# Six column blocks of a gated layer formed while attention still runs, with their results in slots and the score banks in rings of three

## The chip, the cores and the metric

The kernel runs on one core of a Trainium2 chip. The metric is device time in microseconds. The kernel before took 649.47 us as the median of three runs (643.34 to 655.79).

## The reference

```python
scores = 1/sqrt(64) * q @ k.T                  # 2 batches, 12 heads, 448 tokens, 64 wide
attn = softmax(causal(scores)) @ v             # row maximum subtracted, sum + 1e-9
x = attn as 896 tokens x 768
xn = x / sqrt(mean(x * x) + 1e-6) * rms_g
g, val = xn @ w_gate, xn @ w_val               # 768 x 1536, float64
y = (g * sigmoid(g) * val) @ w_out             # 1536 x 768
h = y @ w_in                                   # 768 x 2048
out = maximum(0.01 * h, h) @ w_out2            # 2048 x 768
```

The inputs q, k and v are float32. The weights arrive as float64 and are split on the chip.

## The kernel before, in words

**Attention.** The heads go in twelve pairs; pairs 0 to 5 are the first half of the tokens (b = 0, 448 tokens), pairs 6 to 11 the second (b = 1). For each pair `maxima` forms score products (L281) and VectorE reduces each row block to its maximum (L289); `maxima_rows` transposes the maxima (L315) and sends them through DRAM to one row of `mrow` (L320, L324). Two pairs later `exponents` forms the transposed scores minus the maximum (L339, L343), ScalarE takes the exponential (L364), and GpSimd masks it (L370, L374). `attend` forms the sums of the exponentials (L401, into the bank SM) and the products with v (L386, into the bank AV). The sums travel through DRAM to be inverted on 64 partitions (L423, L427, L431, L434) and come back broadcast (L436, L441); GpSimd multiplies (L448), ScalarE squares (L456), and GpSimd adds the squares up in `acc` (L459). The eight banks of PSUM are two for the maxima (SP), four for the exponents (ST), AV and SM.

**Norm.** `norm(b)`, once per half, sums the squares over partitions on TensorE (L477), takes the power on GpSimd (L493), spreads the result over all partitions by four products (L484), copies it to `rsb` (L500), and scales and splits the six row blocks of the half into a rounded part and a rest (L504, L507, L514 or L510). The two parts are `xn`.

**Weights.** `weight` loads one block of 128 columns as float64 (768 KB, L182, a ring of three buffers `raw`), rebuilds the float32 on ScalarE and VectorE (L187, L188, L190, L192, L194, a ring of two buffers `x`), rounds it (L196), and leaves the rest to GpSimd (L197), in a ring of four `hl`. Every product of the three layers is three passes of 128x128 by 448 columns: rounded by rounded, rounded by rest, rest by rounded (L573, L574, L575).

**The gated layer.** Twelve column blocks fc, each with a weight for g and one for val, are formed for both halves (`gate`: 18 matmuls for one weight and one half). `gate_out` takes Silu (L625), multiplies (L627), rounds (L630) and subtracts (L632) into T. The products of fc 0 and 1 for b = 0 (`EARLY = 2`) stand among the last pairs of attention; their `gate_out` waits for the buffers of attention to be given up (`reopen`), as T lies in that memory. Then come y (L669 and after), G (L699 and after) and the output.

**What sets the order.** `Order.add` takes every step with an engine, a cost, its reads and writes, and a rank. `emit` places steps one after another: on the engine that is free first, the ready step of lowest rank, with 6 added for a change of the matmul mode. The result is one fixed list for each engine, that of SyncE among them, which issues all DMAs. On the chip every engine works its list strictly in order, so a step that waits holds up all steps behind it on its engine.

## Time and profile before

| | before |
|---|---|
| median of three runs | 649.47 us |
| the profiled execution | 649.4 us, its span 647.7 us |
| TensorE busy | 623.2 us, 96% of the span |
| VectorE, ScalarE, GpSimd busy | 393.6, 250.1, 196.1 us |
| mean granted clock of TensorE | 0.968 of full speed |
| bytes moved | 68.24 MB, of which 64.78 MB read |

A profile row for an instruction has its start, its length, engine and line, what it writes and reads, how many of its kind are merged, and in square brackets the idle time of the engine before it with what ended it. A row of the stretches has the stretch, its length, and the busy time and count of each engine, the granted clock of TensorE and the load of the DMA engines.

### The profile page before, as it was taken

How to read it: one execution, taken by the hardware profiler on the slowest of the kernel's cores; microseconds unless marked ns; L12 is line 12 of the kernel's file. 1: busy time of each engine (PE TensorE's matmuls, PEld its weight loads, DVE VectorE, ACT ScalarE, POOL GpSimd, SP SyncE). 2: the span in 40 equal slices, each digit the busy share in tenths (PEclk: the TensorE clock that was granted, in tenths of full speed). 3: DMA queues.
4: the chain of work that ended last, by engine and by line, in shares of the span. 5: the costliest groups of instructions: out<-in, count | busy, mean ns of one | idle time of the engine just before them, and what ended most of it. 6: DMA issues, size and time to landing. Idle time of an engine off the chain costs nothing.

```text
span 647.7 us, 8644 instructions
## 1 busy us (share of the span) xinstructions
PE 623.2 (96%) x3280; PEld 537.4 (83%) x3280; DVE 393.6 (61%) x668; ACT 250.1 (39%) x410; POOL 196.1 (30%) x158
## 2 busy tenths in 40 slices
PE   7987888997999999999999999999999999999997
PEld 4554466566989999999999999999999999999997
DVE  5567443625798776655674554599999883444300
ACT  3564442632543433333333223345554543223210
POOL 0154333843233322223232222232233223232300
PEclk9887876998999999999999999999999999999999
DMA  6353221131145233333233223233233333434000
GB/s 241 126 186 102 83 78 32 30 119 60 50 146 190 104 102 130 112 124 118 97 109 135 98 98 101 95 117 127 99 98 87 125 97 115 140 112 143 29 28 28
DMA packets 20177, 68.24 MB, mean 105 GB/s; under 512 B 5092, under 2 KB 8104, under 8 KB 20136
## 3 DMA queue, kind: packets, MB, share of 16 engines
q1 hardware_dynamic: 20136, 67.70, 31.4%
q8 instruction: 25, 0.41, 0.2%
q14 instruction: 16, 0.13, 0.1%
HBM read 64.78 MB, written 2.91 MB: 105 GB/s over the span
## 4 chain that ended last, share of the span: by engine, by line
PE 90%; DVE 3%; issue 3%; DMA 3%; POOL 1%; ACT 1%; SPq 0%; POOLq 0%; DVEq 0%; ACTq 0%
PE bank L573 25%; PE bank L575 25%; PE bank L574 25%; PE bank L386 4%; PE bank L343 3%; PE bank L401 2%; PE bank L281 2%; PE bank L339 2%; DVE bank L289 1%; DMA st<-sd 1%; PE bank L524 1%; POOL hl L197 1%; DVE x L504 1%; PE bank L484 0%; DMA rb<-rd 0%
## 5 line engine op out<-in xcount | busy, mean ns | idle before, releaser
L197 POOL TENSOR_TENSOR hl<-x,hl 128x768 fp32r<-128x768 f32 (+1 forms) x70 | 138.7, 1981 | 334.8 <-ACT hl L196 329.2
L573 PE MATMUL bank<-xn,hl 128*128 128x448 f32 x288 | 106.9, 371 | 2.2 <-ACT xn L507 1.9
L574 PE MATMUL bank<-xn,hl 128*128 128x448 f32 x288 | 106.3, 369 | 1.3 <-POOL xn L514 0.8
L575 PE MATMUL bank<-xn,hl 128*128 128x448 f32 x288 | 106.1, 368 | 0.8 <-POOL hl L197 0.8
L187 ACT ACTIVATE x<-raw 128x768 f32<-128x768 f32 (+1 forms) x70 | 61.7, 883 | 105.1 <-POOL hl L197 105.1
L188 DVE TENSOR_SCALAR x<-x 128x768 f32<-128x768 f32 (+1 forms) x70 | 39.1, 559 | 93.6 <-ACT x L187 93.6
L192 DVE SCALAR_TENSOR_TENSOR x<-raw,x 128x768 uint32<-128x768 uint32 (+1 forms) x70 | 85.0, 1215 | 2.3
L196 ACT CAST hl<-x 128x768 fp32r<-128x768 f32 (+1 forms) x70 | 56.8, 812 | 53.3 <-PE bank L574 44.9
L574 PE MATMUL bank<-y,hl 128*128 128x448 f32 x192 | 70.1, 365 | 0.0
L573 PE MATMUL bank<-G,hl 128*128 128x448 f32 x192 | 70.1, 365 | 0.0
L575 PE MATMUL bank<-G,hl 128*128 128x448 f32 x192 | 70.1, 365 | 0.0
L573 PE MATMUL bank<-y,hl 128*128 128x448 f32 x192 | 70.1, 365 | 0.0
L575 PE MATMUL bank<-y,hl 128*128 128x448 f32 x192 | 70.1, 365 | 0.0
L574 PE MATMUL bank<-G,hl 128*128 128x448 f32 x192 | 70.1, 365 | 0.0
L194 DVE SCALAR_TENSOR_TENSOR x<-raw,x 128x768 uint32<-128x768 uint32 (+1 forms) x70 | 65.1, 929 | 1.1
L573 PEld LDWEIGHTS bank<-xn,hl 128*128 128x128 f32 x288 | 54.8, 190 | 7.7 <-ACT xn L507 2.1
L289 DVE CUSTOM_DVE_ANT_0 bank<-bank,maskw 112x224 f32<-112x224 f32 (+2 forms) x96 | 42.0, 466 | 31.4 <-PE bank L281 30.2
L574 PEld LDWEIGHTS bank<-xn,hl 128*128 128x128 f32 x288 | 54.6, 190 | 6.6 <-POOL xn L514 1.3
L575 PEld LDWEIGHTS bank<-xn,hl 128*128 128x128 f32 x288 | 54.7, 190 | 5.5 <-POOL hl L197 1.2
L573 PE MATMUL bank<-T,hl 128*128 128x448 f32 x144 | 52.6, 365 | 0.0
L575 PE MATMUL bank<-T,hl 128*128 128x448 f32 x144 | 52.6, 365 | 0.0
L574 PE MATMUL bank<-T,hl 128*128 128x448 f32 x144 | 52.6, 365 | 0.0
(79 smaller groups left out, 927.7 us busy)
## 6 DMA issues: line engine op xcount, KB each, us to landing
raw<-in_out SPq DMA_DIRECT2D x24, 768.0 KB
raw<-in_in SPq DMA_DIRECT2D x16, 768.0 KB
raw<-in_gate SPq DMA_DIRECT2D x12, 768.0 KB
raw<-in_val SPq DMA_DIRECT2D x12, 768.0 KB
qk<-in_qk SPq DMA_DIRECT2D x12, 448.0 KB
v<-in_v SPq DMA_DIRECT2D x12, 256.0 KB
raw<-in_out SPq DMA_DIRECT2D x6, 512.0 KB
out<-sg SPq DMA_DIRECT2D x12, 224.0 KB
```

The lines of the kernel that those rows point to most:

```text
L187: add("ACT", 0.85, lambda: nc.scalar.activation(x[:, :w], tf, AF.Abs), r=[kr], w=[kx], rank=rank)
L188: add("DVE", 0.62, lambda: nc.vector.tensor_scalar(x[:, :w], x[:, :w], LEAST, MOST, ALU.max, ALU.min), r=[kx], w=[kx], rank=rank)
L192: add("DVE", 1.0, lambda: nc.vector.scalar_tensor_tensor(xb, top, 0xC0000000, xb, ALU.bitwise_and, ALU.bitwise_or), r=[kr, kx], w=[kx], ra ...
L194: add("DVE", 1.0, lambda: nc.vector.scalar_tensor_tensor(xb, low, 29, xb, ALU.logical_shift_right, ALU.bitwise_or), r=[kr, kx], w=[kx], ra ...
L196: add("ACT", 0.85, lambda: nc.scalar.copy(hl[:, 0, :w], x[:, :w]), r=[kx], w=[kh], rank=rank)
L197: add("POOL", 1.95, lambda: nc.gpsimd.tensor_tensor(out=hl[:, 1, :w], in0=x[:, :w], in1=f32(hl[:, 0, :w]), op=ALU.subtract), r=[kx, kh], w ...
L289: nc.vector.tensor_tensor_reduce(out=s, in0=s, in1=maskw[:, S - w:S], scale=-1.0, scalar=3.0e38, op0=ALU.add, op1=ALU.min, accum_out=m[:, ...
L343: nc.tensor.matmul(bank[:k1 - kb * P, off:off + w], t[r, 1, kb * P:k1], t[r, 0, kb * P:], start=False, stop=True, skip_group_check=True,)
L386: nc.tensor.matmul(AV[j * D:(j + 1) * D, kb * P:S], vt[:, kb, j], p, start=kb == 0, stop=kb == KB - 1, skip_group_check=True,)
L573: nc.tensor.matmul(o, hi, xh, start=s, stop=False, skip_group_check=True)
L574: nc.tensor.matmul(o, hi, xl, start=False, stop=False, skip_group_check=True)
L575: nc.tensor.matmul(o, lo, xh, start=False, stop=e, skip_group_check=True)
```

## The change

The gated layer forms six column blocks instead of two for the first half of the tokens early (`EARLY = 6`), in the banks 4 and 5, and finishes them at once: their `gate_out` no longer waits for attention's memory, as the six results have slots of their own (`big`), and its last step goes to GpSimd. T and G become lists of such slots of one column block and one half; y overwrites `xn`. To make room, the ring `raw` has two buffers instead of three, the rings of q, k and v four instead of five, and `x32` is a ring of eight blocks of 448 columns. `norm(0)` is issued after pair 6 instead of pair 7, with a lower rank for its scaling. Pairs 0 to 5 use three banks for the maxima and three for the exponents; pairs 6 to 11 two and two, which leaves banks 4 and 5 to the gates. As the ring of split weights holds four, the weights of fc 0 to 3 are loaded and split a second time for b = 1, after fc 11 (`again`): 78 blocks are split instead of 70. The number of products is the same: 2953 rows of TensorE's order before and after.

```diff
-    NRAW, NX, NHL = 3, 2, 4
+    NRAW, NX, NHL = 2, 2, 4
...
-    xn = xyp.tile([P, 2, KD, NT], F32R, tag="xy", name="xn")
-    late = {}
...
+    xn = xyp.tile([P, 2, KD, NT], F32R, name="xn")
+    y = xn
...
+    EARLY = 6
+    NBIG = B * KF2
+    big = [xyp.tile([P, 2, S], F32R, name=f"big{n}") for n in range(EARLY)]
+    sgs = [xyp.tile([P, S], F32, name=f"sg{n}") for n in range(2)]
+    order = [(fc, 0) for fc in range(EARLY)]
+    order += [(fc, b) for fc in range(KF) for b in range(B) if (fc, b) not in order]
+    t_slot = {k: n for n, k in enumerate(order)}
+    unused = list(range(len(order), NBIG)) + list(range(len(order)))
+    g_slot = {(fc, b): unused[fc * B + b] for fc in range(KF2) for b in range(B)}
...
-    for fc in range(KF):
-        queue += [(("g", fc), w_gate[fc]), (("v", fc), w_val[fc])]
+    for fc in list(range(KF)) + list(range(EARLY - 2)):
+        again = len(queue) >= 2 * KF
+        queue += [(("g", fc, again), w_gate[fc]), (("v", fc, again), w_val[fc])]
...
-    NQ, NR, NM, NB = 5, 3, 4, 4
+    NQ, NR, NM, NB = 4, 3, 4, 4
...
-    x32 = ap.tile([P, KD, NT], F32, name="x32")
+    NX32 = 8
+    x32 = ring(NX32, [P, S], F32, "x32_")
...
-    SP, ST, AV, SM = banks[0:2], banks[2:6], banks[6], banks[7]
+    AV, SM = banks[6], banks[7]
...
+    maxima_banks = [0, 1, 2], [0, 1]
+    exponent_banks = [3, 4, 5], [2, 3]
+    taken = {}
+    def take(lists, i):
+        use = lists[i >= NP]
+        n = taken.get((use[0], len(use)), 0)
+        taken[use[0], len(use)] = n + 2
+        return [use[(n + j) % len(use)] for j in range(2)]
...
-            use = [(spn[0] + j) % 2 for j in range(2)]
-            spn[0] += 2
+            use = take(maxima_banks, i)
...
-            use = [(stn[0] + j) % 4 for j in range(2)]
-            stn[0] += 2
+            use = take(exponent_banks, i)
...
-        x = x32[:, hp, b * S:(b + 1) * S]
+        x = x32[i % NX32]
...
-        u0, u1 = stn[0] % 4, (stn[0] + 1) % 4
-        stn[0] += 2
-        B0, B1 = ST[u0], ST[u1]
+        n = 0 if b else 4
+        B0, B1 = banks[n:n + 2]
+        k0, k1 = ("bank", n), ("bank", n + 1)
...
-            x = x32[:, i, b * S:(b + 1) * S]
+            n = (b * NP + i) % NX32
+            x = x32[n]
...
-                r=["rs"], w=[("x", b, i)], rank=rank + i + 30)
+                r=["rs"], w=[("x32", n)], rank=rank + i)
...
+    def bank_key(n):
+        return {6: "av", 7: "sm"}.get(n, ("bank", n))
+    def next_bank():
+        turn[0] += 1
+        return (turn[0] + 5) % 8
+            xh, xl = src(ks, b)
...
+    def of_T(k, b):
+        return [big[t_slot[k, b]][:, e] for e in range(2)]
...
+    def gate(nm, fc, b, rank, bank=None, again=False):
+        gate_bank[nm, fc, b] = u = next_bank() if bank is None else bank
+        product(u, (nm, fc, again), of_xn, six, b, True, True, rank, xn_keys(b))
...
+    def gate_out(fc, b, rank, room, lower):
+        s = next_sg()
+        ug, uv = gate_bank["g", fc, b], gate_bank["v", fc, b]
+        n = t_slot[fc, b]
+        def view(e):
+            return big[n][:, e]
+        add("ACT", 0.57, lambda: nc.scalar.activation(sgs[s], banks[ug][:, :S], AF.Silu),
+            r=[bank_key(ug)], w=[("sg", s)], rank=rank)
+        add("DVE", 0.65, lambda: nc.vector.tensor_tensor(
+            out=sgs[s], in0=banks[uv][:, :S], in1=sgs[s], op=ALU.mult),
+            r=[bank_key(uv)], w=[("sg", s)], rank=rank)
+        add("ACT", 0.57, lambda: nc.scalar.copy(view(0), sgs[s]),
+            r=[("sg", s)] + room, w=[("big", n)], rank=rank)
+        add(*lower, lambda: (nc.gpsimd if lower[0] == "POOL" else nc.vector).tensor_tensor(
+            out=view(1), in0=sgs[s], in1=f32(view(0)), op=ALU.subtract),
+            r=[("sg", s)], w=[("big", n)], rank=rank)
...
-    EARLY = 2
-    HEAD = [k for k, _ in queue[:2 * EARLY]]
-    for n, key in enumerate(HEAD):
-        weight(key, 40.0 + 10 * n, at=20.0 + 8 * n)
+    def early_rank(fc):
+        return 10.0 * (NP + 3 + fc) + 9
+    def early_weights(fc):
+        for n, nm in enumerate("gv"):
+            weight((nm, fc, False), early_rank(fc) - 12, at=40.0 + 8 * (2 * fc + n))
+    for fc in range(NHL // 2):
+        early_weights(fc)
...
-            if i in (NP + 1, NPAIR - 1):
-                norm(i // NP - (i < NPAIR - 1))
...
+            if i == NP:
+                norm(0)
+                for fc in range(EARLY):
+                    for n, nm in enumerate("gv"):
+                        gate(nm, fc, 0, early_rank(fc), bank=4 + n)
+                    gate_out(fc, 0, early_rank(fc) - 10, [], ("POOL", 1.15))
+                    if fc + NHL // 2 < EARLY:
+                        early_weights(fc + NHL // 2)
+    norm(1)
...
+        big.extend(bigp.tile([P, 2, S], F32R, name=f"big{n}") for n in range(EARLY, NBIG))
...
+    held = [k for k in list(od.written) if k not in ("const", ("bank", 4), ("bank", 5))
+            and k[0] not in ("hl", "raw", "x", "big", "sg")]
+    add("X", 0.0, reopen, r=held, w=["room"])
+    for again in (False, True):
+        for fc in range(EARLY - 2) if again else range(EARLY - 2, KF):
+            rank = FF + 2 + fc + (KF if again else 0)
+            kept = fc < EARLY and not again
+            if not kept:
                 for nm in "gv":
+                    weight((nm, fc, again), rank - 1)
+            for b in range(1 if kept or again else 0, B):
+                for nm in "gv":
+                    gate(nm, fc, b, rank, again=again)
+                gate_out(fc, b, rank, ["room"], ("DVE", 0.7))
...
```

The names in the rows of the order are the tiles of the kernel with the number of the buffer; an `ISA` row of L289 or L313 is a reduction to the row maximum, and the one behind it with only `m` reads out its result.

TensorE around the second norm (L484 before, L506 after: the four products that spread the inverse root over the partitions). Before:

```order
L575 MATMUL bank3_76<-xn_81,hl3_72 128x448
L484 MATMUL bank5_78<-dg0_152,ones_147 128x112
L484 MATMUL bank5_78<-dg1_153,ones_147 128x112
L484 MATMUL bank5_78<-dg2_154,ones_147 128x112
L484 MATMUL bank5_78<-dg3_155,ones_147 128x112
L573 MATMUL bank4_77<-xn_81,hl0_69 128x448
```

After, with 45 matmuls on the weights in hl0 to hl3 between the last L506 and the last row, which is the first product of the second half:

```order
L506 MATMUL bank1_73<-dg3_167,ones_159 128x112
L561 MATMUL bank4_76<-xn_80,hl0_68 128x448
...
L563 MATMUL bank4_76<-xn_80,hl2_70 128x448
L561 MATMUL bank5_77<-xn_80,hl3_71 128x448
L562 MATMUL bank5_77<-xn_80,hl3_71 128x448
L563 MATMUL bank5_77<-xn_80,hl3_71 128x448
L561 MATMUL bank6_78<-xn_80,hl0_68 128x448
```

Before, the product behind the spread is one of the second half. Now products of the first half with the blocks fc 4 and 5 stand between.

VectorE at the maxima of pair 4, with steps of a weight's rebuilding (L188, L190) and the inverse of pair 1's sums (L431, L434) between them. Before:

```order
L289 ISA bank1_74,m0_104<-bank1_74,maskw_149 112x336
L289 ISA m0_104 112x1
L188 TENSOR_SCALAR x0_67<-x0_67 128x768
L190 TENSOR_SCALAR x0_67<-x0_67 128x768
L289 ISA bank0_73,m0_104<-bank0_73,maskw_149 112x224
L289 ISA m0_104 112x1
L431 SCALAR_TENSOR_TENSOR r1_131<-st1_127 64x14
L434 RECIPROCAL r1_131<-r1_131 64x14
L289 ISA bank0_73,m0_104<-bank0_73,maskw_149 112x112
```

After, at the maxima of pair 8:

```order
L207 SCALAR_TENSOR_TENSOR x0_66<-raw0_64,x0_66 128x768
L313 ISA bank0_72,m0_109<-bank0_72,maskw_161 112x336
L313 ISA m0_109 112x1
L313 ISA bank1_73,m0_109<-bank1_73,maskw_161 112x336
L313 ISA m0_109 112x1
L209 SCALAR_TENSOR_TENSOR x0_66<-raw0_64,x0_66 128x768
L203 TENSOR_SCALAR x1_67<-x1_67 128x768
L205 TENSOR_SCALAR x1_67<-x1_67 128x768
L207 SCALAR_TENSOR_TENSOR x1_67<-raw1_65,x1_67 128x768
L313 ISA bank0_72,m0_109<-bank0_72,maskw_161 112x224
```

The rebuilding of weights has left the maxima of pairs 0 to 5. Six blocks are now rebuilt between the maxima of pair 6 and the scaling of the first norm, where none was.

ScalarE from the copies of pair 9's products on (L443 copies sums, L468 the products with v, L604 is Silu, L609 the rounding behind it, L386 the exponential, L202 and L211 are steps of a weight). After:

```order
L468 COPY x32_1_150<-bank6_78 128x448
L604 ACT_TABLE_LOAD
L604 ACTIVATE sg1_88<-bank4_76 128x448
L211 CAST hl0_68<-x0_66 128x768
L202 ACTIVATE x0_66<-raw0_64 128x768
L211 CAST hl1_69<-x1_67 128x768
L609 CAST big0_81<-sg1_88 128x448
L386 ACT_TABLE_LOAD
L386 ACTIVATE p0_121<-bank2_74 128x320
L386 ACTIVATE p1_122<-bank3_75 128x320
```

Before, one table load stood ahead of the first Silu, behind all exponentials. Now Silu comes between exponentials: there are five loads at L604 and L386 in place of the one at L625.

## Rows read from the trace of the kernel before

**Rows 1.** Stretches of the span: busy time of each engine, granted clock, DMA load.
```profile
40.00:64.00 24.00, 19.00 (x142) 11.98 (x142) 17.08 (x50) 14.44 (x28) 12.16 (x17) 0.88 0.43 130
64.00:116.00 52.00, 46.33 (x311) 28.94 (x303) 23.35 (x100) 21.55 (x46) 19.58 (x28) 0.79 0.23 66
...
124.00:155.00 31.00, 31.00 (x220) 23.24 (x219) 7.56 (x19) 8.53 (x19) 15.66 (x23) 1.00 0.29 101
155.00:164.00 9.00, 5.73 (x16) 4.11 (x15) 7.42 (x9) 4.88 (x8) 4.46 (x3) 0.62 0.00 0
...
180.00:640.00 460.00, 459.21 (x2266) 425.27 (x2265) 293.95 (x371) 167.84 (x254) 128.74 (x65) 1.00 0.32 108
```

**Rows 2.** Timeline of TensorE around the second norm.
```profile
154.22 1.04 PE L484 MATMUL bank<-dg,ones 112*128 112x112 f32 x8
157.19 0.74 PE L573 MATMUL bank<-xn,hl 128*128 128x448 f32 x1 [1.94 <-ACT xn L507]
...
163.91 0.39 PE L573 MATMUL bank<-xn,hl 128*128 128x448 f32 x1
```

**Rows 3.** Timeline of TensorE in the first half of attention: its waits.
```profile
7.30 2.63 PE L281 MATMUL bank<-qkr 64*112 64x336 f32 x6 [0.91 <-DVE m L289]
...
32.81 0.95 PE L281 MATMUL bank<-qkr 64*112 64x256 f32 x4 [0.66 <-DVE m L289]
...
49.95 0.26 PE L315 MATMUL bank<-ident,m 112*8 112x112 f32 x1 [2.54 <-DVE m L289]
...
62.33 0.35 PE L315 MATMUL bank<-ident,m 112*8 112x112 f32 x1 [2.46 <-DVE m L289]
```

**Rows 4.** Chain of waits: the copy ahead of the first of these two waits.
```profile
43.61 4.81 DMA st<-sd
```

**Rows 5.** Timeline of VectorE ahead of the second of them.
```profile
56.87 1.37 DVE L188 TENSOR_SCALAR x<-x 128x768 f32<-128x768 f32 x1
58.28 1.38 DVE L190 TENSOR_SCALAR x<-x 128x768 uint32<-128x768 uint32 x1
59.69 0.96 DVE L192 SCALAR_TENSOR_TENSOR x<-raw,x 128x768 uint32<-128x768 uint32 x1
```

**Rows 6.** Stretches of 4 us around the two waits.
```profile
48.00:52.00 4.00, 2.05 (x19) 1.27 (x23) 3.42 (x12) 0.75 (x2) 0.63 (x2) 0.91 0.29 75
52.00:56.00 4.00, 4.00 (x30) 1.74 (x22) 0.96 (x5) 1.94 (x3) 1.09 (x1) 0.66 0.50 181
...
60.00:64.00 4.00, 1.67 (x9) 0.69 (x13) 3.83 (x16) 1.30 (x3) 1.55 (x4) 0.69 0.23 23
64.00:68.00 4.00, 4.00 (x24) 1.45 (x18) 1.11 (x6) 0.53 (x1) 2.82 (x2) 0.50 0.46 159
```

**Rows 7.** Groups of instructions on VectorE, shapes apart: busy, mean ns | idle before.
```profile
L192 DVE SCALAR_TENSOR_TENSOR x<-raw,x 128x768 uint32<-128x768 uint32 x64 | 80.9, 1264 | 2.1
...
L194 DVE SCALAR_TENSOR_TENSOR x<-raw,x 128x768 uint32<-128x768 uint32 x64 | 60.9, 952 | 0.9
...
L190 DVE TENSOR_SCALAR x<-x 128x768 uint32<-128x768 uint32 x64 | 39.8, 623 | 1.4
L188 DVE TENSOR_SCALAR x<-x 128x768 f32<-128x768 f32 x64 | 36.6, 572 | 83.4 <-ACT x L187 83.4
...
L627 DVE TENSOR_TENSOR sg<-bank,sg 128x448 f32<-128x448 f32 x24 | 14.9, 620 | 35.5 <-PE bank L575 33.9 <-ACT sg L625 1.6
L632 DVE TENSOR_TENSOR T<-sg,T 128x448 fp32r<-128x448 f32 x24 | 14.8, 616 | 1.5 <-ACT T L630 1.5
```

**Rows 8.** Timeline of ScalarE at the first Silu.
```profile
162.46 0.56 ACT L507 CAST xn<-x 128x448 fp32r<-128x448 f32 x1 [0.57 <-DVE x L504]
163.04 1.28 ACT L625 ACT_TABLE_LOAD   x1
164.34 0.55 ACT L625 ACTIVATE sg<-bank 128x448 f32<-128x448 f32 x1
```

**Rows 9.** Waits of TensorE from 124 us on: total, times, longest.
```profile
PE bank L575 <- POOL hl L197: 0.8, 1, 0.8
```

More of the change, by code (lines that the diff above doesn't have):

```diff
@@ L300, in products @@
                     for j in range(2):
-                        product(j, c, SP[use[j]], 256 * n)
+                        product(j, c, banks[use[j]], 256 * n)
             cost = sum(max(256, (c + 1) * C) * 0.00045 + 0.05 for c in group)
-            add("PE", cost, products, r=[("qkr", i % NR)], w=[("sp", u) for u in use],
+            add("PE", cost, products, r=[("qkr", i % NR)], w=[("bank", u) for u in use],
                 rank=10 * i - 29, mode=64)
```

189 lines of the change are left out of this document (67 added, 122 removed).

## The prediction

> **What bounds the kernel now.** I read the stretches first, then the timeline of TensorE, then what ended its waits. From 180 to 640 us TensorE is busy 459.2 of 460 us at a granted clock of 1.00, with 2266 matmuls: 0.203 us for each [rows 1]. Nothing is to be had there but by fewer matmuls, and their number stays. The stretch from 124 to 155 us, in which the last pairs of attention and the four early products stand, is full too: 31.00 of 31.00 at 1.00 [rows 1]. So the place into which the change puts more early products has no hole. A product that is put there only pushes other work back, and time is won where TensorE idles or runs slowly. That is in two places: the 9 us behind the second norm (5.73 busy, clock 0.62) and the attention ahead of 116 us, with clock 0.88 from 40 to 64 us and 0.79 from 64 to 116 us [rows 1].
>
> **The gap behind the second norm.** The spread ends at 154.22 + 1.04 = 155.26, and at 163.91 the pace is normal again; twelve matmuls lie between [rows 2]. At 0.203 us they need 2.4 of these 8.65 us, so 6.2 us are lost: first waiting for the split rows of the second half, then at the low clock. In the new order 45 products of the first half stand there, 45 x 0.203 = 9.1 us, and the split rows were all used 8.65 us behind the spread. So the cover suffices, narrowly for the last rows and amply for the first, which are wanted first. I take all of it: **-6.2**, with bounds 0 and -6.2 (a spread that is itself late would not shrink it, but a scaling that queues behind a weight on VectorE could leave part).
>
> **The front: what goes.** In the first six pairs TensorE waits four times for a reduction that frees one of the two banks of maxima, 0.66 to 0.91 us, together 3.0 [rows 3]. A third bank, with other products between, takes these away. Then come two longer waits, 2.54 and 2.46 us [rows 3]. Ahead of the first, the inverse of a pair's sums waits on VectorE for a small copy that took 4.81 us [rows 4], and the reductions stand behind it; ahead of the second VectorE works at a weight for 1.37, 1.38 and 0.96 us [rows 5] before it comes to the reduction. After both the clock falls: 0.91 and 0.66, then 0.69 and 0.50 of full speed in stretches of 4 us [rows 6], 0.50 being the level of 1.2 GHz. What this takes is 4 x (0.09 + 0.34) = 1.7 and 4 x (0.31 + 0.50) = 3.2 us. So the first event cost 4.3, the second 5.7, together 10.0 us, with four weights rebuilt in the stretch. Weights now come only from pair 6 on. What goes: 3.0 + 10.0 = 13.0.
>
> **The front: what comes.** Six weights are rebuilt between the maxima of pair 6 and the scaling of the first norm. One takes VectorE 0.572 + 0.623 + 1.264 + 0.952 = 3.41 us [rows 7], six 20.5. From 64 to 116 us VectorE was busy 23.35 of 52 us [rows 1]; with them it is 43.8, or 84%, more than the 17.08 of 24 (71%) of the stretch in which the two events fell. There is room, but not for steps that come in an unlucky order. At the price of before, 10.0 / 4 = 2.5 each, six cost 15.0; only two of the four were followed by such a wait, so a weight may cost nothing. I take the middle, 7.5, since this stretch loses a fifth of its clock already and can't lose the same time twice. The two banks for exponents in pairs 6 to 8, where no gate fills in, I price by the nearest row, a ring of two that makes TensorE wait 0.66 us [rows 3]: 3 x 0.66 = 2.0. The front: -13.0 + 7.5 + 2.0 = **-3.5**, with bounds -13.0 and +4.0.
>
> **Later attention.** Four more table loads come onto ScalarE between the exponentials of the last two pairs; one took 1.28 us [rows 8], four 5.1. Two of them return to the exponential, and at one of these TensorE has little between the products and their use; I take one load: **+1.3**, bounds 0 and 5.1. The row shows the Silu 0.02 us behind the load and the load 0.02 us behind the instruction before. The Trainium skill, "ScalarE: Activation LUTs", section "What ACT_TABLE_LOAD costs", has a drain of 1.38 us with every load, 2.66 us in all; this case's row does not show it, and four such switches would be an estimated 10.6 us of ScalarE in place of 5.1.
>
> Eight loads of weights now stand in SyncE's list among the small copies of pairs 2 to 7, each waiting for VectorE to be done with the block two before. If one holds the copies up as at 43.61 us, it costs 4.3; if the buffer is free in time, nothing. I take half of one: **+2.1**, bounds 0 and 34.
>
> **The gated layer after attention.** One wait of 0.8 us for a weight [rows 9] goes, since the weights are no longer held until attention ends: **-0.8**. Eight blocks are split again. For one such column block VectorE needs 2 x 3.41 + 0.62 + 0.62 = 8.1 us [rows 7], and TensorE 36 x 0.203 = 7.3. The four split blocks in the ring cover the difference; without that cover it would be 4 x 0.8 = 3 us. The ring `raw` of two, the finish on GpSimd and the slots I cost at nothing: ahead of each weight lies 7.3 us of products or more, and in the second half GpSimd was busy 15.66 of 31 us [rows 1].
>
> **The sum**, against the profiled execution's own 649.4 us, which is also the median shown (649.47): 649.4 - 6.2 - 3.5 + 1.3 + 2.1 - 0.8 = 642.3. I forecast **642 us**, 7 us less.
>
> **Rivals.**
> A. *The front becomes dense.* The six weights fit into VectorE's idle time and the later terms vanish: 642.3 - 7.5 - 1.3 - 2.1 = 631. For it: VectorE idled 28.7 of 52 us there. Against it: the same should have held from 40 to 64 us.
> B. *The change does not do what it says.* The early products fill no idle time, because the stretch was full, and the front keeps its length as other waits take over from those that go. Only the gap is won: 642.3 + 3.5 = 646. For it: most of the front's loss lies at 64 to 116 us (52 x 0.21 = 11 us of clock, 5.7 of idle time), where no weight was rebuilt.
> C. *SyncE's list becomes the bound* (slower). In place of the weights' price and the half event, each of the eight loads delays the copies behind it by one event of 4.3: 642.3 - 7.5 - 2.1 + 34 = 667. From the fourth load on that does so the kernel is slower than before, from the seventh by over 2%. For it: one of the four loads of before did this [rows 4]. Against it: no other wait of TensorE from 40 to 64 us ended on a copy.
> D. *Table loads on the path.* If TensorE waits through all four, 642.3 + 5.1 - 1.3 = 646. By the Trainium skill's figure, same page and section, it would be an estimated 652.
>
> **Chances.** The forecast 0.50 (its own range 636 to 649), A 0.20, B 0.15, C 0.10, D 0.05. The range from 630 to 654 leaves out most of C, the low tail of A and little else, about 2 in 10. A measurement of this kernel tells 2% from no change, 13 us: below 636.5 is faster, above 662.5 slower. Faster: nearly all of A and a tenth of the forecast, 0.25. Slower: most of C, 0.08. Within 2%: 0.67.
>
> **What the profile after would show.** The gap: no wait at the first product of the second half, and a clock of 1.00 there. The front: no wait over 1 us at the transposes of pairs 4 and 5, and pair 5 done well before 62 us. The weights' price: VectorE's rebuilding steps ahead of the reductions of pairs 6 to 10, with TensorE waiting behind them. Table loads: ScalarE's row of exponents behind a load, with TensorE's next product waiting for it. I am wrong if the clock in the last four pairs of attention falls below 1.00, for then the fixed order has brought waits into a stretch that had none, or if the front shrinks by more than 13 us.

## The result, and the profile after

The changed kernel takes 652.3 us (median of 14 runs, 649.6 to 660.3); the kernel before took 646.2 beside it (14 runs, 642.5 to 657.0). The ratio is 1.011, with a 95% interval from 1.007 to 1.015: 1.1% slower, where I had forecast 1.1% faster. The comparisons leave disturbed executions out; the profiled ones of e3, e15 and e16 (spans 657.6, 656.5 and 653.2 us) are disturbed, so only the places of waits are read from them.

The profiled execution after took 649.6 us, its span is 647.8 us. It is the fastest of its 14 runs, while that of before (649.4) lies 3 us above its median. The two traces are therefore equally long: they show how time moved from one stretch to another, and not the 6 us by which the medians differ.

The stretches of the kernel after, in the columns of [rows 1], with 148 to 152 us added:

```profile
40.00:64.00 24.00, 20.78 (x161) 11.25 (x161) 13.35 (x43) 12.81 (x24) 8.82 (x13) 0.93 0.53 175
64.00:116.00 52.00, 45.39 (x269) 25.83 (x271) 39.97 (x104) 27.11 (x54) 28.73 (x33) 0.84 0.46 147
124.00:155.00 31.00, 29.30 (x162) 22.03 (x159) 22.57 (x24) 21.90 (x34) 21.25 (x16) 0.94 0.29 94
...
148.00:152.00 4.00, 4.00 (x18) 2.88 (x16) 3.23 (x5) 2.17 (x4) 2.29 (x1) 0.64 0.41 133
...
155.00:164.00 9.00, 9.00 (x59) 6.78 (x58) 5.80 (x8) 4.43 (x7) 6.56 (x7) 1.00 0.30 113
180.00:640.00 460.00, 456.35 (x2250) 422.14 (x2249) 322.50 (x384) 173.16 (x261) 138.97 (x71) 1.00 0.34 112
```

From 124 to 155 us, full at a clock of 1.00 before, TensorE now has waits (29.30 of 31.00) and a clock of 0.94; VectorE has 22.57 us of work there where it had 7.56, ScalarE 21.90 for 8.53. From 180 to 640 us 2.9 us of TensorE are missing against before.

The timeline of TensorE after, some of its waits in the middle of attention and those around the second norm (they answer to [rows 2, 3]):

```profile
49.66 0.41 PE L362 MATMUL bank<-mrow,onesr 64*128 64x320 f32 x1 [1.88 <-ACT p L386]
66.32 0.95 PE L305 MATMUL bank<-qkr 64*112 64x256 f32 x4 [2.61 <-DVE m L313]
...
147.42 0.41 PE L362 MATMUL bank<-mrow,onesr 64*128 64x320 f32 x1 [1.24 <-ACT p L386]
...
167.18 0.95 PE L499 MATMUL bank<-ones,acc 128*112 128x2 f32 x8 [0.32 <-POOL acc L481]
...
174.29 1.15 PE L506 MATMUL bank<-dg,ones 112*128 112x112 f32 x8 [1.79 <-DVE dg L518]
...
185.66 0.47 PE L561 MATMUL bank<-xn,hl 128*128 128x448 f32 x1 [1.71 <-DVE sg L606]
```

The two long waits of [rows 3] are gone from their places; another wait for a reduction stands at 66.32 us, and products of exponents now wait for the exponentials that empty their bank. Behind the spread 42 of the 45 products of the first half run on without a pause, and the half-clock stretch of [rows 2] does not occur. The first product of the second half has no wait. But ahead of the spread TensorE now waits 0.32 and 1.79 us, where it had no wait before. Behind it the 43rd product of the cover itself waits 1.71 us: it is the first with the second weight of fc 5 and goes into bank 5, which holds a product of fc 4 until VectorE's L606 has read it.

**The same by work done.** In the written order 72 products of the early blocks stand ahead of the second spread before, 156 after. At the pace of 0.203 us the 84 more are 17.1 us. So the spread of after is due at 154.22 + 17.1 = 171.3 and comes at 174.29: 3.0 late. From there to the end before took 647.7 - 154.2 = 493.5 us and after 647.8 - 174.3 = 473.5, for 17.1 us less work: 2.9 won, and not the whole 6.2 of the gap. What was won there had been lost ahead of it.

The same reckoning at two earlier points tells where. First the spread of the first norm and the sums of the last pair before:

```profile
108.87 2.05 PE L484 MATMUL bank<-dg,ones 112*128 112x112 f32 x8
...
141.20 1.95 PE L401 MATMUL bank<-p,ones 128*64 128x448 f32 x16
```

Then after:

```profile
103.67 1.15 PE L506 MATMUL bank<-dg,ones 112*128 112x112 f32 x8
...
156.29 1.95 PE L423 MATMUL bank<-p,ones 128*64 128x448 f32 x16
```

At the first norm's spread no early product has run in either kernel, and after is 5.2 us ahead. At the last pair's sums 102 early products stand ahead after and 30 before, 14.6 us more work, and after comes 15.1 us later: 0.5 behind. So the front won time, and pairs 8 to 11 with the norm behind them lost 8.2 us of it again: 5.7 up to the last pair's sums, 2.5 from there to the spread. These are single executions, so the sizes are rough.

VectorE and GpSimd at the second norm show where. First VectorE's timeline after:

```profile
163.05 1.64 DVE L203 TENSOR_SCALAR x<-x 128x768 f32<-128x768 f32 x1
...
167.98 0.96 DVE L209 SCALAR_TENSOR_TENSOR x<-raw,x 128x768 uint32<-128x768 uint32 x1
168.86 0.55 DVE L203 TENSOR_SCALAR x<-x 128x768 f32<-128x768 f32 x1
169.33 0.15 DVE L513 TENSOR_SCALAR ms<-bank 112x4 f32<-112x4 f32 x1
169.44 0.56 DVE L205 TENSOR_SCALAR x<-x 128x768 uint32<-128x768 uint32 x1
170.04 3.47 DVE L207 SCALAR_TENSOR_TENSOR x<-raw,x 128x768 uint32<-128x768 uint32 x1
173.43 0.61 DVE L606 TENSOR_TENSOR sg<-bank,sg 128x448 f32<-128x448 f32 x1
173.97 0.83 DVE L518 TENSOR_SCALAR dg<-ident,rt 112x112 f32<-112x112 f32 x4
...
176.05 5.86 DVE L527 SCALAR_TENSOR_TENSOR x<-x,gsb,rsb 128x448 f32<-128x448 f32 x4
...
185.00 0.61 DVE L606 TENSOR_TENSOR sg<-bank,sg 128x448 f32<-128x448 f32 x1
```

Then GpSimd's of the same kernel:

```profile
162.42 1.85 POOL L212 TENSOR_TENSOR hl<-x,hl 128x768 fp32r<-128x768 f32 x1 [0.62 <-ACT hl L211]
164.24 1.48 POOL L611 TENSOR_TENSOR big<-sg,big 128x448 fp32r<-128x448 f32 x1
165.67 1.46 POOL L481 TENSOR_TENSOR acc<-acc,sq 128x448 f32<-128x448 f32 x1
169.56 1.32 POOL L515 TENSOR_TENSOR rt<-ms,nhalf 112x4 f32<-112x4 f32 x1 [2.43 <-DVE ms L513]
170.86 1.84 POOL L212 TENSOR_TENSOR hl<-x,hl 128x768 fp32r<-128x768 f32 x1
```

The diagonals `dg` need only `rt`, done at 170.88. They start at 173.97, since VectorE's list has two instructions of the last block's weights and one of a gate in between, one of them (L207) 3.47 us long where its like (L209) took 0.96 at 167.98. The L606 for which the cover waits comes at 185.00, since VectorE's list has the scaling of the norm (L527) ahead of it. On GpSimd the last sum (L481) stands behind a weight's low half and a gate's. From the last sum to the spread it is 174.29 - 167.13 = 7.2 us; before, the sum ended at 150.09 by its row below, 4.1 us ahead of the spread. GpSimd of the kernel before:

```profile
148.94 1.15 POOL L459 TENSOR_TENSOR acc<-acc,sq 128x448 f32<-128x448 f32 x1 [2.59 <-ACT sq L456]
151.59 1.02 POOL L493 TENSOR_TENSOR rt<-ms,nhalf 112x4 f32<-112x4 f32 x1 [1.49 <-DVE ms L491]
```

The groups of VectorE after that answer to [rows 7] (mean ns behind the comma): the first and the second are the same instructions as before, 72 in place of 64, and 79 and 179 ns longer each; the third, the scaling, took 830 ns before.

```profile
L207 DVE SCALAR_TENSOR_TENSOR x<-raw,x 128x768 uint32<-128x768 uint32 x72 | 96.7, 1343 | 2.2
L209 DVE SCALAR_TENSOR_TENSOR x<-raw,x 128x768 uint32<-128x768 uint32 x72 | 81.5, 1131 | 1.3
...
L527 DVE SCALAR_TENSOR_TENSOR x<-x,gsb,rsb 128x448 f32<-128x448 f32 x12 | 13.4, 1155 | 0.5 <-ACT rsb L522 0.5
```

The waits of TensorE after from 200 us on answer to [rows 9]; the wait for the weight stays and a second one comes, both where the blocks that are split again end and the output product begins:

```profile
PE bank L562 <- DVE big L611: 1.2, 1, 1.2
PE bank L563 <- POOL hl L212: 0.7, 1, 0.7
```

### The profile page after: what moved, and what is told of

It reads as the page before. It is cut to its first block, busy times and chain, and to the rows that moved or that the text cites. A ratio compares the mean times of both kernels' runs of the same rounds, so it can differ in the third digit from the quotient of the medians.

```text
span 647.8 us, 8738 instructions
## 1 busy us (share of the span) xinstructions
PE 623.4 (96%) x3280; PEld 532.1 (82%) x3280; DVE 447.3 (69%) x694; ACT 268.8 (41%) x430; POOL 226.9 (35%) x172
## 4 chain that ended last, share of the span: by engine, by line
PE 75%; DVE 11%; DMA 6%; ACT 3%; issue 2%; POOL 2%; SPq 1%; ACTq 0%; DVEq 0%; POOLq 0%
PE bank L561 22%; PE bank L562 22%; PE bank L563 22%; PE bank L366 2%; DVE x L207 2%; PE bank L423 2%; PE bank L408 2%; DMA st<-sd 2%; DVE x L527 2%; DMA rb<-rd 1%; DVE x L203 1%; DVE x L209 1%; PE bank L362 1%; PE bank L305 1%; DVE x L205 1%
## 5 line engine op out<-in xcount | busy, mean ns | idle before, releaser
L212 POOL TENSOR_TENSOR hl<-x,hl 128x768 fp32r<-128x768 f32 (+1 forms) x78 | 156.8, 2011 | 311.1 <-ACT hl L211 302.8
L561 PE MATMUL bank<-xn,hl 128*128 128x448 f32 x480 | 177.1, 369 | 1.7 <-DVE sg L606 1.7
L563 PE MATMUL bank<-xn,hl 128*128 128x448 f32 x480 | 175.8, 366 | 0.0
L562 PE MATMUL bank<-xn,hl 128*128 128x448 f32 x480 | 175.7, 366 | 0.0
L562 PE MATMUL bank<-big,hl 128*128 128x448 f32 x336 | 122.9, 366 | 1.2 <-DVE big L611 1.2
L563 PE MATMUL bank<-big,hl 128*128 128x448 f32 x336 | 122.9, 366 | 0.7 <-POOL hl L212 0.7
L561 PE MATMUL bank<-big,hl 128*128 128x448 f32 x336 | 122.7, 365 | 0.0
L202 ACT ACTIVATE x<-raw 128x768 f32<-128x768 f32 (+1 forms) x78 | 69.1, 886 | 122.8 <-POOL hl L212 83.9
L203 DVE TENSOR_SCALAR x<-x 128x768 f32<-128x768 f32 (+1 forms) x78 | 49.8, 638 | 81.8 <-ACT x L202 81.8
L207 DVE SCALAR_TENSOR_TENSOR x<-raw,x 128x768 uint32<-128x768 uint32 (+1 forms) x78 | 100.8, 1293 | 2.4
L561 PEld LDWEIGHTS bank<-xn,hl 128*128 128x128 f32 x480 | 90.3, 188 | 11.9 <-issue 2.7
L563 PEld LDWEIGHTS bank<-xn,hl 128*128 128x128 f32 x480 | 90.4, 188 | 7.2
L562 PEld LDWEIGHTS bank<-xn,hl 128*128 128x128 f32 x480 | 90.4, 188 | 6.9
L209 DVE SCALAR_TENSOR_TENSOR x<-raw,x 128x768 uint32<-128x768 uint32 (+1 forms) x78 | 85.6, 1098 | 1.4
L211 ACT CAST hl<-x 128x768 fp32r<-128x768 f32 (+1 forms) x78 | 63.6, 815 | 53.1 <-PE bank L562 36.4
L562 PEld LDWEIGHTS bank<-big,hl 128*128 128x128 f32 x336 | 63.1, 188 | 6.5 <-DVE big L611 1.6
L563 PEld LDWEIGHTS bank<-big,hl 128*128 128x128 f32 x336 | 63.1, 188 | 6.0 <-POOL hl L212 1.1
L561 PEld LDWEIGHTS bank<-big,hl 128*128 128x128 f32 x336 | 63.1, 188 | 5.0
L313 DVE CUSTOM_DVE_ANT_0 bank<-bank,maskw 112x224 f32<-112x224 f32 (+2 forms) x96 | 41.7, 466 | 20.4 <-PE bank L305 18.0
L205 DVE TENSOR_SCALAR x<-x 128x768 uint32<-128x768 uint32 (+1 forms) x78 | 46.4, 595 | 1.8
L729 DVE TENSOR_TENSOR big<-sg,big 128x448 fp32r<-128x448 f32 x32 | 45.6, 1424 | 0.0
L366 PE MATMUL bank<-qk 64*128 64x448 f32 (+3 forms) x192 | 44.5, 435 | 0.0
```

The costliest lines, as they stand in the source:

```text
L202: add("ACT", 0.85, lambda: nc.scalar.activation(x[:, :w], tf, AF.Abs), r=[kr], w=[kx], rank=rank)
L203: add("DVE", 0.62, lambda: nc.vector.tensor_scalar(x[:, :w], x[:, :w], LEAST, MOST, ALU.max, ALU.min), r=[kx], w=[kx], rank=rank)
L205: add("DVE", 0.6, lambda: nc.vector.tensor_scalar(xb, xb, 3, 0x3FFFFFF8, ALU.logical_shift_left, ALU.bitwise_and), r=[kx], w=[kx], rank=rank)
L207: add("DVE", 1.0, lambda: nc.vector.scalar_tensor_tensor(xb, top, 0xC0000000, xb, ALU.bitwise_and, ALU.bitwise_or), r=[kr, kx], w=[kx], ra ...
L209: add("DVE", 1.0, lambda: nc.vector.scalar_tensor_tensor(xb, low, 29, xb, ALU.logical_shift_right, ALU.bitwise_or), r=[kr, kx], w=[kx], ra ...
L211: add("ACT", 0.85, lambda: nc.scalar.copy(hl[:, 0, :w], x[:, :w]), r=[kx], w=[kh], rank=rank)
```

## The experiments

Ratios are to the kernel before, run in turn on the same chip, with 95% intervals; the changed kernel stands at 1.011.

### The split of the banks

**e1**, the kernel before with rings of three:

```diff
-    SP, ST, AV, SM = banks[0:2], banks[2:6], banks[6], banks[7]
+    SP, ST, AV, SM = banks[0:3], banks[3:6], banks[6], banks[7]
...
-            use = [(spn[0] + j) % 2 for j in range(2)]
+            use = [(spn[0] + j) % 3 for j in range(2)]
...
-            use = [(stn[0] + j) % 4 for j in range(2)]
+            use = [(stn[0] + j) % 3 for j in range(2)]
...
```

> The kernel before with one part of the change: three banks for the maxima and three for the exponents, for all pairs, in place of two and four. Theory R (the rings cost the time): 1.005 or more of before, with ScalarE's exponentials as the releaser of TensorE's waits in attention. Theory V (VectorE and the extra weight work cost the time; the rings help the front by the 3 us that I forecast): 0.995, the waits on reductions in pairs 0 to 5 gone.

Measured 654.9 us, 1.013 (1.009 to 1.017): slower, by about as much as the whole change. TensorE's timeline at the second norm, where the kernel before has no wait:

```profile
153.95 0.95 PE L477 MATMUL bank<-ones,acc 128*112 128x2 f32 x8 [4.16 <-POOL acc L459]
156.64 2.05 PE L484 MATMUL bank<-dg,ones 112*128 112x112 f32 x8 [1.74 <-DVE dg L496]
```

**e6**, exponents in three banks, maxima in two:

```diff
-            use = [(stn[0] + j) % 4 for j in range(2)]
+            use = [(stn[0] + j) % 3 for j in range(2)]
```

> The kernel before with a ring of three banks for exponents in place of four; maxima keep two, and the sixth bank stands empty until attention ends. It parts the two halves of the run with rings of three. If the exponents' missing bank is the cost: as with both rings of three, ratio 1.010 to 1.016, about 654 us. If the third bank of maxima is the cost (maxima are then done sooner and the exponents' turn comes later): no difference from before, 646 us. If the third bank of maxima gave back what I reckoned with, 3 us, this run is 3 us slower than with both rings of three, 658.

Measured 649.1 us, 1.004 (1.001 to 1.008), about a third of e1's cost. So the third bank of maxima, which I had booked as 3.0 us won, wins nothing here. But its price cannot be read from the difference, since both edits also move the early products in the written order. Between the last pair's sums and the second spread the kernel before has 42 of them, e6 has 15 and e1 only 3; 18 stand behind the spread in both. The waits of e1 shown above, and two of 1.72 and 1.74 us at the same places in e6, stand where the kernel before has these products.

**e7**, two banks for exponents in pairs 6 to 11:

```diff
-            use = [(stn[0] + j) % 4 for j in range(2)]
+            use = [(stn[0] + j) % (4 if i < NP else 2) for j in range(2)]
```

> The kernel before with two banks for exponents in pairs 6 to 11 (four stay in pairs 0 to 5); the norms use the two banks that come free. Theory R: the pairs of the second half then wait behind exponentials as the changed kernel with two early blocks does (12.8 us of waits in all), some 10 us slower, 656 us. Rival (the gap between the changed kernel with two early blocks, 665, and the rings of three, 655, comes from slots, weights and order): no more than 3 us slower, 649.

Measured 651.4 us, 1.009 (1.006 to 1.013), between the two. No wait for exponentials is among the seven largest of its trace, so theory R (some 10 us) has the size too high and the place wrong, and the rival (at most 3 us) has it too low.

**e5**, the changed kernel with two and four in the first half:

```diff
-    maxima_banks = [0, 1, 2], [0, 1]
-    exponent_banks = [3, 4, 5], [2, 3]
+    maxima_banks = [0, 1], [0, 1]
+    exponent_banks = [2, 3, 4, 5], [2, 3]
```

> The changed kernel with one edit: in the first six pairs the banks are split as before, two for maxima and four for exponents; pairs 6 to 11 keep two and two. Theory R (the time is lost where a product waits for the exponentials that empty its bank, and in the first half the ring of three does it): the 8.5 us that rings of three cost the kernel before come back, about 644 us, 1% under the changed kernel's 652, and the waits behind exponentials in the first half (1.88, 0.80, 0.76, 1.08 us) are gone. Theory V (VectorE is what is late, with six weights and the scaling on it): the split of the banks in the first half matters little, within 2 us of 652.

Measured 663.0 us, 1.027 (1.022 to 1.031): 10 us slower than the changed kernel, against both. The waits of its TensorE (total, times, longest):

```profile
PE bank L362 <- DMA mrow<-md: 8.8, 6, 2.9
PE bank L338 <- DVE m L313: 4.7, 4, 1.5
PE bank L305 <- DVE m L313: 3.2, 6, 0.9
```

The waits for exponentials are not among these, as R said; in their place the exponents wait for the row of maxima. That this row is written later because its products have two banks is likely and not shown. Theory R falls. Rings of three cost 1.3% in the one order, for all pairs (e1), and win about as much in the other, for pairs 0 to 5.

### How many early blocks, and where

**e2** and **e8**, two and four blocks in place of six:

```diff
-    EARLY = 6
+    EARLY = 2      # e8: 4
```

> The change with two column blocks early in place of six (EARLY = 2), so no weight is split twice and only four are split before the second norm; slots, rings and the early finish stay. Theory V: the time comes back to that of before or better, 0.995 to 1.002 of it, and VectorE is busy under 75% from 155 to 200 us. Theory R: it stays at 1.01 of before.

> The changed kernel with four early column blocks in place of six (two of them split again and not four). Two early blocks gave 665 us, six 652. If each early block fills idle time alike: halfway, less 1.2 us for the two blocks that are not split again, 657. If it is the last two blocks, those behind the second norm, that win: 664. If four are enough to fill what is idle, 651, since the two blocks more only cost a split each.

Measured 665.2 us, 1.031 (1.027 to 1.035), against both theories, and 656.8, 1.017 (1.011 to 1.023), halfway, as the first expectation had it. In e2 all 72 products stand ahead of the last pair's sums, and TensorE's timeline there reads:

```profile
148.64 0.41 PE L362 MATMUL bank<-mrow,onesr 64*128 64x320 f32 x1 [2.07 <-ACT p L386]
...
164.96 1.65 PE L499 MATMUL bank<-ones,acc 128*112 128x2 f32 x8 [5.62 <-POOL acc L481]
168.28 2.05 PE L506 MATMUL bank<-dg,ones 112*128 112x112 f32 x8 [1.67 <-DVE dg L518]
```

The kernel before has the same 72 but ranks them last, so that 42 stand between the last pair's sums and the spread. In the new order they are used up ahead of these sums; only further blocks cover the end. From two to six blocks the time falls 13 us.

**e10**, four blocks and five buffers for the loads:

```diff
-    EARLY = 6
+    EARLY = 4
...
-    NQ, NR, NM, NB = 4, 3, 4, 4
+    NQ, NR, NM, NB = 5, 3, 4, 4
```

> The changed kernel with four early blocks, and five buffers for the pairs' loads as before, which fit then; against the run with four early blocks and four buffers, 656.8 us. Theory M: 3 to 8 us less, 649 to 654. Rival: no difference, 657.

Measured 654.1 us, 1.014 (1.010 to 1.018), 1.6 us less than e8 by the ratios, with overlapping intervals: undecided.

**e11**, each block one pair later:

```diff
-        return 10.0 * (NP + 3 + fc) + 9
+        return 10.0 * (NP + 4 + fc) + 9
```

> The changed kernel with each early block placed one pair later: in the written order 123 products stand ahead of the second norm's spread in place of 156, and 93 behind it in place of 60. Theory P (what counts is that products are left for the serial steps around the second norm; the last pairs have enough without them): the gap is covered wholly, the waits behind the spread (1.7 us and the slow stretch) go, 649 us. Rival (the pairs 8 to 10 need the products, since each of their steps waits for ScalarE or VectorE): the waits in these pairs grow by more than the 3 us won, 655.

Measured 652.5 us, 1.011 (1.008 to 1.014): no difference. With 93 products behind the spread the wait of the cover for bank 5 falls to 0.6 us, another of 0.7 us comes at 221.59 us, and the sum waits 3.1 us for GpSimd ahead of the spread.

### The small terms

**e3**, no second split:

```diff
-            if not kept:
+            if not kept and not again:
```

> The change without the second splitting of the weights of column blocks 0 to 3: the products for b = 1 read whatever stands in the ring, so these blocks are wrong, and eight loads and splits are left out after the gates. Theory V in its first form (the second split itself costs): 3 us or more less than the change, ratio to before 1.005. If the second split costs only the wait of 1.9 us seen at 320 to 340 us: ratio 1.008.

Measured 649.7 us, 1.007 (1.004 to 1.011): 2.4 us less by the ratios, with overlapping intervals. The two waits behind 200 us shown above (1.2 and 0.7) are not there.

**e4**, no table loads during attention:

```diff
-        add("ACT", 0.57, lambda: nc.scalar.activation(sgs[s], banks[ug][:, :S], AF.Silu),
+        add("ACT", 0.57, lambda: nc.scalar.activation(sgs[s], banks[ug][:, :S], AF.Silu if room else AF.Copy),
```

> The change with a plain copy in place of Silu in the six early blocks (their result is wrong), so that no table is loaded between the exponentials. By the row of 1.28 us for each of four loads, of which TensorE saw at most 2.5 us of waits on exponentials: 2 us less than the change, ratio 1.008. If the loads hold up the whole chain of the last pairs: 5 us less, ratio 1.003.

Measured 656.1 us, 1.016 (1.012 to 1.021): nothing won. One load (145.53 us, 1.28) does stand ahead of the exponentials for which TensorE waits at 147.42, but without it the sum waits 6.0 us for GpSimd (at 169.44). The edit leaves the order of every engine as it is. So one written order can have its waits around the norm in different places: 0.32, 1.79 and 1.71 us in the profiled execution after, 6.0, none and 0.9 here.

**e9**, the smaller memories in the kernel before:

```diff
-    NRAW, NX, NHL = 3, 2, 4
+    NRAW, NX, NHL = 2, 2, 4
...
-    NQ, NR, NM, NB = 5, 3, 4, 4
+    NQ, NR, NM, NB = 4, 3, 4, 4
```

> The kernel before with the changed kernel's smaller memories alone: four buffers in place of five for a pair's loads, two in place of three for raw weights; banks, early blocks and order rules as before. Theory M (the loads are asked for later, and the small copies behind them in SyncE's list come later too): 3 to 8 us slower than before, 649 to 654, with more waits of exponents for their row of maxima. Rival (the loads lead by far more than a buffer): within 2 us of before, 646.

Measured 647.8 us, 1.004 (1.000 to 1.007): 2.5 us by the ratio, between the two expectations, and the interval (0.2 to 4.7 us) reaches into both. Undecided.

### The weights at the second norm

**e12**, diagonals on ScalarE:

```diff
-            add("DVE", 0.25, lambda c=c: nc.vector.tensor_scalar(
-                dgs[c], ident[:C, :C], rt[:, c:c + 1], None, ALU.mult),
+            add("ACT", 0.3, lambda c=c: nc.scalar.activation(
+                dgs[c], ident[:C, :C], AF.Copy, scale=rt[:, c:c + 1]),
```

> The changed kernel with the four diagonals of each norm formed by ScalarE and not by VectorE, where at the second norm they stood behind weights. Theory V (VectorE, crowded by the last blocks' weights, holds up the second norm): the wait of 1.8 us ahead of the spread goes, 650.5 us. Rival: VectorE still has the scaling behind the same weights, the wait moves to the first split rows, 652.

Measured 654.2 us, 1.015 (1.011 to 1.020). The spread waits 2.1 us for ScalarE now, and the cover 2.3 us for bank 5, which L606 on VectorE empties: the wait ahead of the spread did not go, and it did not move to the split rows either. The edit changes the first norm too, and the order from there on (168 early products stand ahead of the second spread), so it shows only that taking this one small step off VectorE wins nothing.

**e13** and **e14**, without the weights of the last four or the last two early blocks:

```diff
     def early_weights(fc):
+        if fc >= 2:      # e14: 4
+            return
```

> The changed kernel, where of the six early blocks only the first two have their weights loaded and split during attention; the other four form their products with the weights that already stand in the ring (their values are wrong by this, and eight splits of weights are left out altogether). Products, banks and order of TensorE stay. Theory V (the weights' rebuilding on VectorE and GpSimd delays the reductions and the second norm): the front gains what the six weights cost and the waits around the second norm (3.8 us) go: 640 us. Rival (the split of banks and the order of the products cost, not the weights): 650 to 653.

> The same with the weights of the first four blocks rebuilt, and only the last two blocks' left out, those that VectorE and GpSimd split around the last pair and the second norm. Theory V, with the cost at the norm: the waits of 0.3, 1.8 and 1.7 us around the second norm go and the last pair is done sooner, 647. With the cost in pairs 6 to 9 instead: 651. Rival: 652.

Measured 645.5 us, 1.003 (0.9995 to 1.006), and 645.0 us, 1.001 (0.999 to 1.004). **Leaving out the last two blocks' four weights takes away the whole difference to the kernel before**; leaving out four more gives nothing further. The edit takes loads and ScalarE's steps away too, and it lets six more products stand behind the spread in e14, so it shows the price of the weights and not which engine takes it. VectorE of e14 around the norm:

```profile
168.24 0.16 DVE L513 TENSOR_SCALAR ms<-bank 112x4 f32<-112x4 f32 x1 [4.44 <-PE bank L499]
169.54 0.84 DVE L518 TENSOR_SCALAR dg<-ident,rt 112x112 f32<-112x112 f32 x4 [1.14 <-POOL rt L515]
...
172.89 3.37 DVE L527 SCALAR_TENSOR_TENSOR x<-x,gsb,rsb 128x448 f32<-128x448 f32 x4 [1.97 <-ACT rsb L522]
```

The three steps of the norm shown find VectorE idle, and TensorE goes through the sum, the spread and the cover without a wait:

```profile
171.25 1.04 PE L506 MATMUL bank<-dg,ones 112*128 112x112 f32 x8
```

By the work done (150 early products ahead of the spread) it comes 1.2 us late in place of 3.0, and 4.7 us are won behind it in place of 2.9. Still e14 is only as fast as the kernel before, where I had forecast 7 us less. So the weights explain why the change is slower, and not all of what the forecast missed.

**e17** and **e18**, work of the last blocks moved from GpSimd to VectorE (e17 the weights' low halves; e18 also the outputs' of three blocks, by the last two lines):

```diff
-        add("POOL", 1.95, lambda: nc.gpsimd.tensor_tensor(
+        here = key in [(nm, fc, False) for nm in "gv" for fc in range(4, EARLY)]
+        add("DVE" if here else "POOL", 1.0 if here else 1.95, lambda: (nc.vector if here else nc.gpsimd).tensor_tensor(
...
-                    gate_out(fc, 0, early_rank(fc) - 10, [], ("POOL", 1.15))
+                    gate_out(fc, 0, early_rank(fc) - 10, [], ("POOL", 1.15) if fc < 3 else ("DVE", 0.7))
```

> The changed kernel, in which the low halves of the last two blocks' four weights are formed by VectorE (about 0.95 us each) and not by GpSimd (1.85 us each). If VectorE's instructions run long because GpSimd works beside them (up to 3.47 us for one that takes 0.96 alone, and some 9 us in all from 158 to 187 us), four of its subtractions gone save more than the 3.8 us that they add: 649. If VectorE's own work is what is late there: 3.8 us more of it, 654 to 656.

> The same, and the low halves of the outputs of blocks 4 to 6 too, 0.62 us each on VectorE in place of 1.15 to 2.4 us on GpSimd. If GpSimd beside it is the cost: 647 to 648, and the sums of the last two pairs on GpSimd no longer stand behind such work. If VectorE's own work is: 656.

Measured 649.4 us, 1.006 (1.003 to 1.009), and 648.7 us, 1.006 (1.003 to 1.010). With 3.8 us more work on VectorE the kernel is about 3 us faster than the change by the ratios. The intervals just overlap (the change 1.007 to 1.015), so the size is uncertain; the 654 to 656 us of the other theory are out. VectorE of e17 at the norm:

```profile
171.15 0.16 DVE L514 TENSOR_SCALAR ms<-bank 112x4 f32<-112x4 f32 x1
171.23 0.55 DVE L205 TENSOR_SCALAR x<-x 128x768 uint32<-128x768 uint32 x1
171.94 0.62 DVE L607 TENSOR_TENSOR sg<-bank,sg 128x448 f32<-128x448 f32 x1 [0.16 <-PE bank L564]
172.48 0.95 DVE L213 TENSOR_TENSOR hl<-x,hl 128x768 fp32r<-128x768 f32 x1
173.35 1.73 DVE L519 TENSOR_SCALAR dg<-ident,rt 112x112 f32<-112x112 f32 x4
175.00 0.94 DVE L207 SCALAR_TENSOR_TENSOR x<-raw,x 128x768 uint32<-128x768 uint32 x1
```

The instruction of 3.47 us takes 0.94 here, and TensorE reaches the spread without a wait, at the sum too:

```profile
175.39 1.04 PE L507 MATMUL bank<-dg,ones 112*128 112x112 f32 x8
```

Behind it remain two waits, 1.0 and 0.5 us, in place of 1.71. By the ratios, GpSimd's part of the last weights then costs roughly half of their price. Whether it costs by making VectorE's instructions beside it long or by holding up GpSimd's own list (the last sum stood behind a low half there) these runs do not part, and what makes up the other half is open.

### Cover behind the norm, by itself

**e15** and **e16**, the kernel before with 36 or 18 of its own early products held behind the spread:

```diff
-        add("PE", 0.95, spread, r=[("dg", c) for c in range(NC)], w=[("st", u1)], rank=rank - 20, mode=128)
+        add("PE", 0.95, spread, r=[("dg", c) for c in range(NC)], w=[("st", u1), "spread"], rank=rank - 20, mode=128)
...
-            gate(nm, fc, 0, FF + fc)
+            gate(nm, fc, 0, FF + fc, ["spread"] if fc else [])      # e16: if fc and nm == "v"
...
```

The lines left out hand this list on to the products.

> The kernel before, in which the 36 products of its second early block wait for the second norm's spread, and so stand behind it; nothing else is changed. If products behind the norm are worth what I put (6.2 us) and the norm's steps ahead of it had more cover than they need: 640 us. If the last pair and the norm need all 72 as cover: the gap behind the spread goes and as much comes ahead of it, 646 or a little more.

> The same with only the last 18 products of the kernel before held behind the spread. They are 3.7 us of cover against a gap of 6.2 us: 643 us if nothing is lost ahead of the norm; 646 if the chain ahead of the norm sets the time.

Measured 647.3 us, 1.004 (1.000 to 1.007), and 644.3 us, 0.999 (0.996 to 1.003): nothing won. TensorE of e15:

```profile
148.46 1.38 PE L477 MATMUL bank<-ones,acc 128*112 128x2 f32 x8 [3.83 <-POOL acc L459]
151.57 2.05 PE L484 MATMUL bank<-dg,ones 112*128 112x112 f32 x8 [1.74 <-DVE dg L496]
```

No wait is left behind the spread, and two open ahead of it, 3.83 + 1.74 = 5.6 us in this profile, against the 6.2 that the gap was. No version that ran is measurably faster than the kernel before.

## Why the prediction was wrong

The step that failed is the gap: "So the cover suffices, narrowly for the last rows and amply for the first, which are wanted first. I take all of it: -6.2", with its bound "a scaling that queues behind a weight on VectorE could leave part". Behind the spread I had -6.2 and -0.8, 7.0 us, and the traces have 2.9. Ahead of it my terms came to almost nothing (-3.5 + 1.3 + 2.1), and the traces have 3.0 us lost. These 7 us are the half of the miss that the two traces hold; the other 6 lie between the profiled executions and the medians. The step failed in three ways.

**The weights that make the cover had a price, and I put none on it.** I priced six weights, those between pair 6 and the first norm's scaling. The change has twelve in attention; the last four are rebuilt exactly where the last pair and the second norm run. e14 puts them at 1.011 - 1.001 of 646, about 6 us: as much as the gap was worth, with the other sign. Of the six that I did price, at 7.5, e13 leaves out two, and two others besides; that won nothing more. I saw VectorE's free time over whole stretches (84% busy) and not the place where one instruction ahead of another holds up a chain. "The ring `raw` of two, the finish on GpSimd and the slots I cost at nothing" had GpSimd's busy time over a stretch as its reason, and fails with e17 in the same way.

**The cover needs VectorE too.** I counted 45 products and took them to run on by themselves. The 43rd needs a bank that VectorE empties, and VectorE's list has the norm's scaling ahead of that: the wait of 1.71 us. My sign for the gap, no wait at the first product of the second half, came true all the same.

**A gap behind a chain is not free time by itself.** In e15 and e16 nothing was won by moving products behind the spread (1.004 and 0.999), and the places of the waits say why: what closes on one side opens on the other. Additional products cover both sides in e14, but 36 of them need two weights, each with four steps on VectorE and a low half on GpSimd, at the very moment at which the norm needs both.

Why the change without these four weights (e14) is still not 7 us faster than the kernel before is not settled. By the ratios the second split is 2.4 us of it (e3) and the smaller memories 2.5 (e9), with intervals that leave room for much less. "A product that is put there only pushes other work back" did not hold either: from the first norm to the last pair's sums after loses the 5.7 us shown above.

The other terms, in the order of the sum:
- The front, -3.5. At the spread of the first norm after is 5.2 us ahead in these two profiles, more than I had put, and the lead is gone at the second. The reasons given do not hold singly: in the order of before, rings of three win nothing (e1, e6), and in the new order they are worth 10 us (e5). Single profiles can't settle single microseconds here: in e7, whose edit starts at pair 6, the clock of the first 20 us is 0.69 where that of before is 1.00.
- Table loads, +1.3: nothing to be had without them (e4). Rival D is out. The Trainium skill, "ScalarE: Activation LUTs", section "What ACT_TABLE_LOAD costs", has a further drain of 1.38 us with every load; the load at 145.53 us takes 1.28 and the exponentials start at 146.82, so this trace shows no time between them.
- SyncE's list, +2.1: e13 loads four weights fewer than e14 during attention and takes the same time, and the smaller memories cost 0.4% (e9, its interval from 0.0 to 0.7%). Rival C, the slower one that I gave 0.10, did not occur; the kernel became slower by another mechanism, which I had as a bound of the gap and not as a rival with a price. Rival B, in which the early products fill no idle time, comes nearest, but it still had the whole gap won.
- The weight's wait, -0.8: it stays at 0.7.
- The second split, 0, or 3 without cover: 2.4 (e3, with overlapping intervals). The cover was not there: the second halves alone give 36 products for two weights, and the waits of 1.2 and 0.7 us stand at the end of them.
- The base: the profiled 649.4 was some 3 us over the median of 14 runs, 646.2. By that the same sum would have forecast 639, further off.

My own mark for being wrong, a clock below 1.00 in the last four pairs, came true: 0.94 from 124 to 155 us, with 0.64 from 148 to 152.

What stays open besides is why rings of three cost 1.3% in one order and win 1.5% in the other. e5 shows which wait takes over, and e1 that the early products had moved away from the norm; neither gives a rule for when.

## What to carry to other kernels

Work put into a gap must be followed back through every engine that prepares it: here TensorE's cover was bought with VectorE and GpSimd time on the very chain that it was to cover, and it needed VectorE once more to empty its banks. Move the existing filler first (e15, e16): if the wait only changes sides, the chain is the limit and not the gap. An effect of one part measured in one order can change its sign in another, so parts should be undone in the changed kernel as well as done in the old one.

## What was unexpected of the hardware

VectorE's instructions with two inputs in memory run long beside GpSimd: 3.47 us at 170.04 us for one that takes 0.94 in e17, and it ends at 173.51, 0.8 us behind the end (172.70) of GpSimd's subtraction, as if it had started only then. In the trace after, none of the 51 instructions of L207 that overlap no tensor instruction of GpSimd takes over 0.97 us; of the 27 that do, the longest are these 3.47 us. The gates' product L606, one input of which is a bank, takes 615 ns on the mean, before 620 [rows 7]. The Trainium skill, "SBUF — State Buffer", section "Who interferes with whom", says that a VectorE instruction with two inputs in this memory contends with a GpSimd one that reads it, and that the port they share is an exclusive lock; these rows agree with it. Two inputs are not needed for it: L203 has one, and took 1.64 us at 163.05, beside GpSimd's L212, and 0.55 at 168.86, where GpSimd was idle.

The kernel before has long instructions too (1264 ns on the mean, L192 in [rows 7]). With four weights on the path, taking their low halves off GpSimd made the kernel some 3 us faster (e17).
